# Phase integers summed in PSUM, transforms in 64x64 blocks, finer transposes and a new order, in a gated mix of S4D convolution and GLU

## The chip, the cores and the metric

One core of a Trainium2 chip runs the kernel. The metric is device time in microseconds (us). Before the change three runs took 764.48, 769.40 and 765.78 us; the median is 765.78.

## The reference

The input u is 2048 positions x 448 channels. Two branches read it, and a gate per position mixes them.

```python
# branch A: a state space model as a long convolution
dt = jnp.exp(log_dt)
A = -jnp.exp(log_A_real) + 1j * A_imag          # [448, 256]
C = (C_real + 1j * C_imag) * dt[:, None]
P = jnp.exp((A * dt[:, None])[:, :, None] * pos[None, None, :])
K = 2.0 * jnp.einsum("dn,dnl->dl", C, P).real   # [448, 2048]
Kf = jnp.fft.rfft(K, L2); Uf = jnp.fft.rfft(u_t, L2)
y = jnp.fft.irfft(Uf * Kf[None, :, :], L2)[:, :, :L]
a = y.transpose(0, 2, 1) + u * D_skip
# branch B: a gated linear unit, F = 1792
b = (sigmoid(x @ w_gate) * (x @ w_up)) @ w_down
g = sigmoid((u * gate_w).sum(-1, keepdims=True))
out = g * a + (1 - g) * b
```

In the kernel x of branch B is the same u.

## The kernel before

Everything is written as a list of operations, each with its engine, an estimated cost, the tiles that it reads and writes, and a priority. A planner (`Plan.order`) then simulates the five queues with these costs and hands out, at each moment, the ready operation of lowest rank; the table `RANK` overrides the priority for an engine, a tile name and a stage, and a tuple spreads several values over the operations of one kind. The result is a fixed program for each queue: TensorE (PE), VectorE (DVE), ScalarE (ACT), GpSimd (POOL) and SyncE (SP), which issues nearly all transfers in that order.

**GLU.** Weights and inputs are split into a rounded part (fp32r) and a remainder, and each product is three matmuls (L1180 to L1185 up, L1197 to L1199 down). ACT makes the rounded parts (L1154) and the tanh (L1168), DVE the remainders (L1156, L1172), the gating (L1169) and the running sum (L1213). This work depends on little else, so the planner uses it to fill PE during all stages.

**K.** For 28 chunks of 16 channels (`kgen`), `half_chunk` makes phases, cosines, sines and powers, and contracts them over the 256 states on PE in four column strips (L1075). In `turns` (L1002) PE turns six rows of phase digits into turns with a 96x128 by 512 matmul (L1010), ACT rounds them by adding and subtracting a large number (L1020, L1021, tile nn), and the integers are taken off. In this kernel PE does the first matmul a second time as the start of a new sum in the same PSUM bank, and adds nn through an identity matrix (L1025). ACT then takes the absolute value and the sine from the bank.

**Convolution.** A `Chain` (L551) holds one half of the channels (224) as x, 128 partitions x 32 x 224. Four of them run: two for u, whose spectra `us` go to DRAM, and two for K. Each has a first stage with twiddles (`stage1`, L599), a transposition of 32x32 blocks (by DRAM for three chains, by DVE for the last, L613), and a second stage. The second stage goes pair by pair (`spectrum_pair`, L624): four matmuls of 128 rows to 64 columns and 224 moving columns (L631), with a matrix that holds two 64x64 blocks and zeros. For u, ACT copies the result to x. For K, `product_pair` (L657) multiplies it with u's spectrum, loaded pair by pair into `ua`, on DVE into `ub` (L660), subtracts and adds the complex parts (L665, L666), and makes the inverse of the second stage with 64 rows to 128 columns (L674); ACT copies that to x. After another transposition, `back` (L680) makes the last matmuls (L711) and adds the result, times the gate, to the GLU's (L715). The tile pool of the products, `fk`, opens only when K's pool is done, so both chains of K have their products after the last chunk of K, in the last 200 us.

The matrices of the second stage, with a line each for the old forward and inverse blocks:

```python
m = np.zeros((128, 384), np.float32)
m[re, kr], m[im, kr] = cw, sw
m[kr, ir], m[ki, ir] = cw, -sw
```

Of the kernel before, what the change touches and what calls it, by code (L numbers as in the profile page):

```python
# [29 lines left out]
    ('Act', 'aci', 10): 301.5,  # L30
    ('Act', 'acr', 10): 451.5,
    ('Act', 'acr', 19): 236.5,
    ('Act', 'ci', 10): -166,
    ('Act', 'ci', 19): -194,
    ('Act', 'dots', 2): 332,
    ('Act', 'ec', 20): (66, -97, 126.5, 20, 20, 122.5, 20, 49.5),
    ('Act', 'ex1', 10): 1,
    ('Act', 'ex1', 19): 79,
    ('Act', 'fr', 20): (83.5, 83.5, -162, 49, 105, 90, 90, 20),
    ('Act', 'fx', 30): 244,  # L40
    ('Act', 'fx', 40): 275,
    ('Act', 'hh', 5): (5, -38.5, -38.5, 233, 233),
    ('Act', 'hh', 21): (108.5, 21, 21, -12, -12, -12),
    ('Act', 'hh', 45): 250,
    ('Act', 'hi', 10): -56.5,
    ('Act', 'nn', 20): (20, -251, -142.5, -142.5, -19, -247.5, 66, -161.5),
    ('Act', 'sg', 5): (5, 5, 310.5, 310.5, 5),
    ('Act', 'sg', 21): 99,
    ('Act', 'sg', 45): -123.5,
    ('Act', 'th0', 10): 264.5,  # L50
    ('Act', 'th0', 19): 194,
    ('Act', 'vh', 5): -355,
    ('Act', 'wh', 21): 139,
    ('Act', 'wh', 45): 123.5,
    ('Act', 'xs', 5): -263,
    ('DVE', 'aci', 19): -179.5,
    ('DVE', 'acr', 19): 545,
# [27 lines left out]
    ('DVE', 'uax', 40): (40, -67),  # L85
    ('DVE', 'ubx', 40): 250,
# [1240 lines left out]
```

## Time and profile before

| | us, or share |
|---|---|
| median of three runs | 765.78 |
| lowest, highest run | 764.48, 769.40 |
| span of the profiled execution, first to last instruction | 763.4 |
| VectorE idle in the span | 106.2 |
| ScalarE idle in the span | 234.1 |
| share of 16 DMA engines' span that queue q1's packets took | 54.9% |

The profile gives the span of its execution and no other time of it; the runs' times hold what lies before the first and after the last instruction as well. Busy times add up an engine's instructions where they do not overlap. On TensorE instructions overlap in its pipeline, so a mean duration there is longer than what one instruction takes from the engine. A row of the page's groups names line, engine, operation, written tile <- read tiles, shape and count, then busy us and mean ns of one, then the idle time ahead of them and who ended it.

### The profile page before, as it was taken

What the parts mean: (1) busy time and instruction counts of PE and PEld (TensorE: products, weight loads), DVE (VectorE), ACT (ScalarE), POOL (GpSimd) and SP (SyncE); (2) the same over time, 40 slices, a digit from 0 to 9 for tenths busy, and PEclk for the clock granted to TensorE, in tenths of its full rate; (3) what the DMA queues carried; (4) which work ended last, traced back from release to release, by engine and by line L of the source; (5) the groups of instructions that cost most, each with busy time, mean ns of one, the idle gap of its engine ahead of it and who ended that gap; (6) DMA issues with size and microseconds to landing.
All of it is one profiled execution on the core that took longest, in us unless ns stands there. A gap on an engine that the chain in (4) does not pass through costs nothing.

```text
span 763.4 us, 17397 instructions
## 1 busy us (share of the span) xinstructions
PE 728.4 (95%) x6996; PEld 552.5 (72%) x6996; DVE 657.2 (86%) x903; ACT 529.3 (69%) x994; POOL 231.4 (30%) x282
## 2 busy tenths in 40 slices
PE   4999999999999999999999999999998979999976
PEld 3878887777876877786677777778786757776743
DVE  5999898999999999999798989999964487677795
ACT  5579466899899899999899998898932513322100
POOL 0033225545554443435447535564000000000000
PEclk9999999999999999999999999999999999999998
DMA  8848417634882645596871359020149612335946
GB/s 274 207 114 221 126 50 208 156 116 142 191 160 107 197 127 179 199 195 183 281 190 62 123 165 183 20 77 14 39 94 235 206 43 73 122 121 152 196 133 168
DMA packets 97960, 111.59 MB, mean 146 GB/s; under 512 B 31032, under 2 KB 84984, under 8 KB 97368
## 3 DMA queue, kind: packets, MB, share of 16 engines
q1 hardware_dynamic: 97624, 110.03, 54.9%
q8 instruction: 55, 0.90, 0.5%
q0 software_dynamic: 256, 0.46, 0.2%
q14 instruction: 25, 0.20, 0.1%
HBM read 74.22 MB, written 36.24 MB: 145 GB/s over the span
## 4 chain that ended last, share of the span: by engine, by line
PE 63%; DMA 14%; DVE 8%; ACT 8%; POOL 2%; SPq 2%; issue 2%; DVEq 0%; ACTq 0%; POOLq 0%
PE gu_gps L1180 7%; PE gu_gps L1181 6%; PE gu_gps L1182 6%; PE dn_gps L1197 5%; DMA fx_fu<-shf 5%; PE tp_egp L1010 5%; PE kp_egp L1075 5%; PE dn_gps L1198 4%; PE dn_gps L1199 4%; PE fps_fups L631 4%; DVE fx_fk L613 2%; SPq L498 2%; PE gu_gps L1184 2%; PE gu_gps L1185 2%; PE tp_egp L1025 2%; PE fps_fups L599 2%
## 5 line engine op out<-in xcount | busy, mean ns | idle before, releaser
L1180 PE MATMUL gu_gps<-xs_glu,wh_glu 128*128 128x512 f32 x336 | 136.4, 406 | 15.3 <-ACT wh_glu L1154 10.5
L1181 PE MATMUL gu_gps<-xs_glu,wh_glu 128*128 128x512 f32 x336 | 133.1, 396 | 0.0
L1182 PE MATMUL gu_gps<-xs_glu,wl_glu 128*128 128x512 f32 x336 | 132.8, 395 | 0.0
L1049 DVE TENSOR_TENSOR es_eg<-tb_eg 128x1024 f32<-128x1024 f32 x112 | 110.1, 1001 | 10.8 <-PE kp_egp L1075 7.0
L1010 PE MATMUL tp_egp<-pos_sb,ph_eg 96*128 96x512 f32 x224 | 93.7, 429 | 1.1 <-ACT fr_eg L1028 0.6
L1197 PE MATMUL dn_gps<-vh_glu,hh_glu 128*128 128x448 f32 x224 | 88.0, 393 | 2.0 <-DVE ob_glu L1213 1.8
L1180 PEld LDWEIGHTS gu_gps<-xs_glu,wh_glu 128*128 128x128 f32 x336 | 64.0, 191 | 33.7 <-ACT wh_glu L1154 10.5
L996 POOL TENSOR_TENSOR tb_eg<-tb_eg 128x96 f32<-128x96 f32 (+2 forms) x84 | 83.9, 1003 | 6.2
L1198 PE MATMUL dn_gps<-vh_glu,hl_glu 128*128 128x448 f32 x224 | 82.4, 368 | 0.9 <-DVE hl_glu L1172 0.8
L1199 PE MATMUL dn_gps<-vl_glu,hh_glu 128*128 128x448 f32 x224 | 82.0, 366 | 0.0
L1021 ACT ACTIVATE nn_eg<-fr_eg 128x512 fp32r<-128x512 f32 x112 | 74.6, 666 | 5.8 <-PE tp_egp L1025 5.4
L1027 ACT ACTIVATE ec_eg<-tp_egp 128x512 f32<-128x512 f32 x112 | 70.3, 630 | 8.0 <-PE tp_egp L1025 7.5
L1182 PEld LDWEIGHTS gu_gps<-xs_glu,wl_glu 128*128 128x128 f32 x336 | 63.9, 190 | 14.9 <-DVE wl_glu L1156 0.5
L1181 PEld LDWEIGHTS gu_gps<-xs_glu,wh_glu 128*128 128x128 f32 x336 | 64.0, 191 | 11.9
L1028 ACT ACTIVATE fr_eg<-tp_egp 128x512 f32<-128x512 f32 x112 | 70.5, 630 | 2.0 <-PE tp_egp L1025 1.9
L1069 DVE TENSOR_TENSOR es_eg<-fr_eg,es_eg 128x1024 f32<-128x1024 f32 x56 | 71.3, 1274 | 0.1
L1067 DVE TENSOR_TENSOR ec_eg<-ec_eg,es_eg 128x1024 f32<-128x1024 f32 x56 | 70.8, 1264 | 0.2
L1168 ACT ACTIVATE sg_glu<-gu_gps 128x512 f32<-128x512 f32 x56 | 34.3, 613 | 50.0 <-PE gu_gps L1185 49.8
L1020 ACT ACTIVATE fr_eg<-tp_egp 128x512 f32<-128x512 f32 x112 | 65.3, 631 | 2.9 <-DVE es_eg L1069 2.0
L986 POOL MEMSET tb_eg<- 128x96 f32 x28 | 7.8, 286 | 193.9 <-DVE es_eg L1049 190.3
L1042 ACT ACTIVATE ec_eg<-ec_eg,half_pi 128x1024 f32<-128x1024 f32 x56 | 66.1, 1180 | 0.2
L1213 DVE SCALAR_TENSOR_TENSOR ob_glu<-dn_gps,og,ob_glu 128x448 f32<-128x448 f32 x72 | 48.8, 678 | 12.0 <-PE dn_gps L1199 11.9
(158 smaller groups left out, 1528.7 us busy)
## 6 DMA issues: line engine op xcount, KB each, us to landing
shf<-fx_fu SPq DMA_DIRECT2D x16, 896.0 KB
fx_fu<-shf SPq DMA_DIRECT2D x16, 896.0 KB
xr_glu<-in_w_dram SPq DMA_DIRECT2D x52, 256.0 KB
us<-fx_fu SPq DMA_DIRECT2D x4, 1792.0 KB
vr_glu<-in_w_dram SPq DMA_DIRECT2D x28, 224.0 KB
gt_pre<-in_u_dram SPq DMA_DIRECT2D x8, 448.0 KB
fx_fu<-in_u_dram SPq DMA_DIRECT2D x16, 224.0 KB
kd<-ke_eg SPq DMA_DIRECT2D x8, 448.0 KB
```

The costliest lines, as they stand in the source:

```text
L996: pool(96 * m, lambda n=n, m=m: G.tensor_mul(g3(n + 1, m), g3(1, m), g3(n, 1).to_broadcast([128, 32, 3, m])))
L1010: T.matmul(tp.real, ph[:, c % 2, 128 * nh:128 * nh + 128].bitcast(F32R), pos[:, 512 * i:512 * i + 512], start=True, stop=last)
L1021: op("Act", c_act(512), lambda: S.activation(nn.real, fi(), AF.Copy, scale=-1.0, bias=MAGIC), [(fr, i)], [nn], prio)
L1049: V.tensor_mul(o.rearrange("p d (i k) -> p d i k", k=ny), x.unsqueeze(3).to_broadcast([128, 16, nx, ny]), y.unsqueeze(2).to_broadcast([128 ...
L1067: op("DVE", c_dve(1024), lambda: V.tensor_mul(ec[:, :, 32:96], ec[:, :, 32:96], es[:, :, 32:96]), [(es, 1), (es, 2)], [(ec, "p")], prio)
L1069: op("DVE", c_dve(1024), lambda: V.tensor_mul(es[:, :, 32:96], fr.real, es[:, :, 32:96]), [fr], [(es, 1), (es, 2)], prio)
L1180: T.matmul(p.real, wh[:, k, cs], x[:, k], start=(k == 0), stop=False)
L1181: T.matmul(p.real, wh[:, k, cs], x[:, 4 + k], start=False, stop=False)
L1182: T.matmul(p.real, wl[:, k, cs], x[:, k], start=False, stop=False)
L1197: T.matmul(p[:, :D], hh[:, ts], vh.real, start=(i == 0), stop=False)
L1198: T.matmul(p[:, :D], hl[:, ts], vh.real, start=False, stop=False)
L1199: T.matmul(p[:, :D], hh[:, ts], vl.real, start=False, stop=(i == len(fs) - 1))
```

## The change

Five things change.

- `turns`: the second run of L1010 is gone. The first matmul's bank is kept, and the identity matmul adds nn onto it.
- The second stage takes two pairs at a time: four matmuls of 64 rows to 64 columns with 448 moving columns, each in its own quarter of the array, into two banks. The matrix shrinks from 128x384 to 128x192.
- The product loads u's spectrum with the real parts on both halves of the rows (c = 0) and the imaginary parts likewise (c = 1), multiplies in place, and lets the inverse matmuls add the two with a turned matrix. `ub`, the subtraction and the addition are gone. Four transfers of 224 KB load a group of two pairs, where two loaded it before. `ua` has 2 buffers instead of 3.
- The transposition on VectorE runs in 8 pieces of 28 channels instead of 4 of 56.
- The planner's costs change (64x64 blocks, column operands, POOL, some matmuls), and `RANK` grows from 84 entries to one for nearly each kind of operation.

```diff
-SU = dict(ft=1, ua=1, ub=1)
-SX = {'ft': 1, 'ua': 3, 'ub': 1, 'fps': 2}
-SK = {'ft': 2, 'ua': 3, 'ub': 1, 'fps': 3}
+SU = dict(ft=1)
+SX = {'ft': 1, 'ua': 2, 'fps': 2}
+SK = {'ft': 2, 'ua': 2, 'fps': 3}
...
+    re, im = slice(0, 32), slice(32, 64)
+    m = np.zeros((2, 64, 3, 64), np.float32)
+    fwd, inv, turned = m[0, :, 0], m[0, :, 1], m[0, :, 2]
+    fwd[re, re], fwd[im, re], fwd[re, im], fwd[im, im] = cw, sw, -sw, cw
+    inv[re, re], inv[im, re], inv[re, im], inv[im, im] = cw, -sw, sw, cw
+    turned[re], turned[im] = inv[im], -inv[re]
+    m[1] = m[0]
+    m = m.reshape(128, 192)
...
+def c_mm64(n, count=1):
+    return [(FOURTHS, 1.6667 * n + 30.0)] * count
...
-                for b in range(4):
+                for b in range(8):
                     def f(b=b):
-                        v = x[:, :, 56 * b:56 * b + 56].rearrange("p l d -> p d l")
+                        v = x[:, :, 28 * b:28 * b + 28].rearrange("p l d -> p d l")
                         V.transpose(v, v)
...
-        def spectrum_pair(self, r):
-            p = self.psum()
+        def spectrum_four(self, b):
+            p = [self.psum(), self.psum()]
             def f():
-                for c in range(2):
+                for z in range(2):
                     for i in range(2):
-                        T.matmul(p[64 * i:64 * i + 64, c * HD:c * HD + HD], m_sb[:, 64 * c:64 * c + 64],
-                                 self.x[:, 2 * r + i], start=True, stop=True)
+                        rows, to = slice(64 * i, 64 * i + 64), slice(64 * (i ^ z), 64 * (i ^ z) + 64)
+                        T.matmul(p[z][to, :D], m_sb[rows, 0:64], self.pair(2 * b + z, rows), start=True, stop=True)
...
-            for r in range(16):
-                ua = self.tile("ua", (128, 2, HD))
-                dma(lambda ua=ua, r=r: ua.real, lambda r=r: us[:, 2 * r:2 * r + 2], 128 * 2 * HD * 4,
-                    [(us, r // 8)], [ua], self.prio)
+            for b in range(8):
+                ua = self.tile("ua", (128, 2, 2, D))
+                for c in range(2):
+                    for g in range(2):
+                        dma(lambda ua=ua, c=c, g=g: ua[64 * g:64 * g + 64, c].rearrange("p z f -> p (z f)"),
+                            lambda b=b, c=c, g=g: us[64 * g + 32 * c:64 * g + 32 * c + 32, 4 * b:4 * b + 4].rearrange(
+                                "k l d -> k (l d)").unsqueeze(0).to_broadcast([2, 32, 2 * D]),
+                            64 * 2 * D * 4, [(us, b // 4)], [(ua, (c, g, 0)), (ua, (c, g, 1))], self.prio, HALF)
...
-            op("DVE", c_dve(2 * D, False), lambda: V.tensor_mul(
-                ub.real, ua.real.unsqueeze(2).to_broadcast([128, 2, 2, HD]),
-                p[:, :D].rearrange("p (c d) -> p c d", c=2).unsqueeze(1).to_broadcast([128, 2, 2, HD])), [ua, p], [ub], prio)
-            def add():
-                V.tensor_sub(x[:, 2 * r], ub[:, 0, 0], ub[:, 1, 1])
-                V.tensor_add(x[:, 2 * r + 1], ub[:, 0, 1], ub[:, 1, 0])
+            for z in range(2):
+                op("DVE", c_dve(2 * D, False), lambda z=z: V.tensor_mul(
+                    ua[:, :, z], ua[:, :, z], p[z][:, :D].unsqueeze(1).to_broadcast([128, 2, D])),
+                   [p[z]], [(ua, (c, g, z)) for c in range(2) for g in range(2)], prio)
...
-                        T.matmul(z[i][:, :HD], m_sb[rows, 128 + 128 * c:256 + 128 * c], x[rows, 2 * r + c],
-                                 start=c == 0, stop=c == 1)
+                    for z in range(2):
+                        for i in range(2):
+                            rows, to = slice(64 * i, 64 * i + 64), slice(64 * (i ^ z), 64 * (i ^ z) + 64)
+                            T.matmul(y[z][to, :D], m_sb[rows, 64 + 64 * c:128 + 64 * c], ua[rows, c, z],
+                                     start=c == 0, stop=c == 1)
-            for i in range(2):
-                evac(lambda i=i: x[:, 2 * r + i], z[i], [(x, r)], prio, HD)
+            for z in range(2):
+                evac(lambda r=2 * b + z: self.pair(r), y[z], [(x, 2 * b + z)], prio)
...
-        def x(last):
-            T.matmul(tp.real, ph[:, c % 2, 128 * nh:128 * nh + 128].bitcast(F32R),
-                     pos[:, 512 * i:512 * i + 512], start=True, stop=last)
-        op("PE", c_mm(512), lambda: x(True), [ph, pos], [tp], prio)
+        op("PE", c_mm(532), lambda: T.matmul(
+            tp.real, ph[:, c % 2, 128 * nh:128 * nh + 128].bitcast(F32R), pos[:, 512 * i:512 * i + 512], start=True, stop=True),
+           [ph, pos], [tp], prio)
...
-        def g():
-            x(False)
-            T.matmul(tp.real, idn.real, nn.real, start=False, stop=True)
-        op("PE", c_mm(512, 2), g, [nn, idn, ph, pos], [tp], prio)
+        op("PE", c_mm(532), lambda: T.matmul(tp.real, idn.real, nn.real, start=False, stop=True, skip_group_check=True),
+           [nn, idn], [tp], prio)
```

More of the change, by code (lines that the diff above doesn't have):

```diff
@@ L86 @@
-    ('DVE', 'ubx', 40): 250,
[27 rows of a table removed]
+    ('Act', 'aci', 10): (-502.5, -363.5),
+    ('Act', 'aci', 19): (-352, 754.5),
+    ('Act', 'acr', 10): (264.5, -368.5, 327),
+    ('Act', 'acr', 19): (729, -700, 800),
+    ('Act', 'ai', 10): -534,
+    ('Act', 'ai', 19): 764,
+    ('Act', 'bsx0', 10): (666, 876),
+    ('Act', 'bsx0', 19): (782, 900),
+    ('Act', 'ci', 10): (689, 173.5, 70),
+    ('Act', 'ci', 19): (25, -391.5, -252.5),
+    ('Act', 'cr', 10): -40,
+    ('Act', 'cr', 19): 549.5,
+    ('Act', 'dots', 1): -419,
@@ new lines @@
+    ('Act', 'dots', 2): -700,
+    ('Act', 'dots', 16): (-78.5, 29),
[14 rows of a table added]
+    ('Act', 'junk', 10): (-404, 388.5),
+    ('Act', 'junk', 19): (-233, -242, -215),
[28 rows of a table added]
+    ('DVE', 'aci', 10): -159.5,
+    ('DVE', 'aci', 19): 19.5,
+    ('DVE', 'acr', 10): -438,
+    ('DVE', 'acr', 19): 655.5,
+    ('DVE', 'ai', 10): -223,
+    ('DVE', 'ai', 19): -40.5,
+    ('DVE', 'bsx0', 10): (-179.5, -174.5),
+    ('DVE', 'bsx0', 19): (-613, 104.5),
+    ('DVE', 'ci', 10): -339,
+    ('DVE', 'ci', 19): -673.5,
+    ('DVE', 'cr', 10): (-561, -429),
@@ L114 @@
+    ('DVE', 'gt', 2): (-301, -580, -690, -614),
+    ('DVE', 'gt', 16): (-169, 813.5, 353, 163.5, -700, -492, 381, 232.5),
+    ('DVE', 'half_pi', 0): 300,
[20 rows of a table added]
+    ('DVE', 'ones', 10): -119.5,
[6 rows of a table added]
+    ('DVE', 'skip', 20): 888,
[5 rows of a table added]
+    ('DVE', 'uax', 40): (840.5, 515, -52, 130.5, -446, -688, 378.5, 896.5),
[26 rows of a table added]
+    ('Pool', 'idn', 1): -436.5,
+    ('Pool', 'pos_sb', 10): 465,
[57 rows of a table added]
 }
 WB, ECB, FRB, TPB, KPB, GUB, FPS, SGB, XRB = 3, 2, 2, 2, 1, 2, 2, 3, 5
-SU = dict(ft=1, ua=1, ub=1)
+SU = dict(ft=1)
 XR0 = 7
 MOVE = True
-SX = {'ft': 1, 'ua': 3, 'ub': 1, 'fps': 2}
@@ L520, in gated_mix @@
     skip = const([128, 2, 56], "skip")
-    m_sb = const([128, 384], "m_sb")
+    m_sb = const([128, 192], "m_sb")
     half_pi = const([128, 1], "half_pi")
@@ L676, in product_pair @@
-            op("PE", c_mm4(HD, 2, ROWS), f, [(x, r), m_sb], z, prio)
-            for i in range(2):
-                evac(lambda i=i: x[:, 2 * r + i], z[i], [(x, r)], prio, HD)
+                    for z in range(2):
[3 more added lines that the diff above has]
+                                     start=c == 0, stop=c == 1)
@@ L1212, in glu_down @@
         o = ob[H, j]
-        op("DVE", c_dve(D, False), lambda: V.scalar_tensor_tensor(
+        op("DVE", c_dve(D, False, column=True), lambda: V.scalar_tensor_tensor(
             o.real, p[:, :D], og[:, c:c + 1], o.real, op0=ALU.mult, op1=ALU.add), [p, (og, c)], [o], prio)
```

97 lines of the change are left out of this document (33 added, 64 removed), and 210 rows, old and new, of the table RANK.

## The prediction

> **What bounds the kernel now.** I read the page first, then the busy time of each engine by stage, then the chain of waits and the order of time on TensorE. The page:
>
> ```profile
> span 763.4 us, 17397 instructions
> ## 1 busy us (share of the span) xinstructions
> PE 728.4 (95%) x6996; PEld 552.5 (72%) x6996; DVE 657.2 (86%) x903; ACT 529.3 (69%) x994; POOL 231.4 (30%) x282
> ```
>
> TensorE leaves 35 us of 763.4 idle, so an instruction taken from it is worth about its pace there, as long as other work can move up. Whether it can is told by the stages: start, parameters, generation of K (140 to 564 us), and the tail with the two inverse transforms. Columns: stretch, its length, then busy us (and count) of PE, PE weight loads, DVE, ACT, POOL, then granted clock, DMA share, GB/s.
>
> ```profile
> 0.00:20.00 20.00, 9.52 (x32) 7.40 (x33) 11.52 (x31) 11.70 (x19) 1.46 (x6) 1.00 0.89 275
> 20.00:140.00 120.00, 118.89 (x541) 99.17 (x540) 110.13 (x197) 80.70 (x146) 39.10 (x42) 1.00 0.59 152
> 140.00:564.00 424.00, 419.39 (x5317) 317.82 (x5316) 399.62 (x473) 388.42 (x714) 190.84 (x234) 1.00 0.53 139
> 564.00:764.00 200.00, 180.62 (x1112) 128.08 (x1110) 135.91 (x204) 48.46 (x117) 0.00 (x0) 0.97 0.57 145
> ```
>
> In the K stage PE is full (419.4 of 424), but VectorE is close behind: 399.6, only 24.4 us of room. In the tail PE has 19.4 us of holes and DVE 64 us of room. The pace of a matmul is not its duration (they overlap); it is the distance of starts, read from the order of time on PE (start, us, instruction):
>
> ```profile
> 157.79 0.40 PE L1010 MATMUL tp_egp<-pos_sb,ph_eg 96*128 96x512 f32 x1
> 158.03 0.40 PE L1025 MATMUL tp_egp<-nn_eg,idn 128*128 128x512 f32 x1
> 158.27 0.40 PE L1184 MATMUL gu_gps<-xs_glu,wh_glu 128*128 128x512 f32 x1
> ```
>
> Each 512-column matmul takes PE 0.24 us. For the small f32 matmuls the chain of waits gives whole groups (start, time that the group holds PE):
>
> ```profile
> 224.58 1.66 PE fps_fups L631 x16
> 227.37 1.03 PE kp_egp L1075 x64
> 228.40 0.91 PE fps_fups L631 x8
> ...
> 580.68 5.21 DMA uax_fk<-us
> ...
> 634.79 0.96 PE fps_fups L674 x8
> ```
>
> Eight records of L631 are one pair of the second transform stage: four matmuls of 224 columns, two records each. One pair alone holds PE 0.91 us; the second of two adds 1.66 - 0.91 = 0.75. So 0.16 goes into entering and leaving the tiling, and 0.75 us is two rounds of 224 columns with two column halves at work.
>
> **The change part by part.** Counts first (busy us, mean ns):
>
> ```profile
> L1010 PE MATMUL tp_egp<-pos_sb,ph_eg 96*128 96x512 f32 x224 | 93.7, 429 | 1.1 <-ACT fr_eg L1028 0.6 <-ACT ec_eg L1027 0.3 <-ACT fr_eg L1020 0.2
> ...
> L631 PE MATMUL fps_fups<-fx_fu,m_sb 128*64 128x224 f32 x384 | 44.3, 363 | 2.0 <-DMA ph_eg<-phd 0.7 <-DMA fx_fu<-shf 0.7 <-ACT fx_fu L549 0.5
> ...
> L674 PE MATMUL fps_fups<-fx_fu,m_sb 64*128 64x224 f32 x128 | 16.2, 372 | 3.7 <-DVE fx_fu L665 3.7
> L674 PE MATMUL fps_fkps<-fx_fk,m_sb 64*128 64x224 f32 x128 | 15.6, 362 | 0.0
> L631 PE MATMUL fps_fkps<-fx_fk,m_sb 128*64 128x224 f32 x128 | 15.3, 360 | 0.0
> ```
>
> 1. *Phase integers.* 112 tiles of turns run L1010 twice, once to round and once more, to be added to L1025. The second goes: 112 x 0.24 = 26.9 us of PE, all in the K stage. No wait is added: L1025 waited for ScalarE's nn before, and the bank was held from the first matmul to the sine before too.
>
> 2. *Second stage in 64x64 blocks.* (384 + 128) / 8 = 64 pairs cost between 64 x 0.83 (two together) = 53.1 and 64 x 0.91 = 58.2; I take 55. Now two pairs are one group of four matmuls of 448 columns, each on its own quarter of the array. If the four run at once, a group is one round of 448 columns, 0.75 + 0.16 = 0.91: 32 x 0.91 = 29 us, a gain of 26. If only two run at once: 1.66 each, 53.1, a gain of 0 to 5, say 2. If none overlap, 3.16 each, 101, a loss of 46. No row shows the quarters. The nearest for the good end is L1075: 32 matmuls of 64 columns in 1.03 us; at 0.75/448 us a column they would take 3.4 us one by one and 0.86 four at a time, so four column strips do run at once. L674 shows two row halves at once (its four matmuls of 224 columns in 0.96). As both axes overlap alone, I take four at once.
>
> A rule of the Trainium skill speaks against it: "TensorEngine Tiling (Array Packing)", Restrictions and Gotchas, says that different row tiles cannot access the same PSUM bank simultaneously, and here the upper and lower rows of one group write halves of one bank. No run here shows what the chip does then; by this rule the second price above would hold, and the sum would be that of rival B.
>
> 3. *Inverse.* 64 x 128 blocks become 64 x 64. 32 pairs x 0.96 = 30.7 us before; 16 groups of two rounds, 1.50 + 0.21 = 1.71, are 27.4 after: a gain of 3.3; two at a time 3.21, 51.4, a loss of 20.7.
>
> So PE loses 26.9 + 26 + 3.3 = 56 us. Half the pairs (the transforms of u) lie in the K stage: 26.9 + 13 = 40 there, 16 in the tail.
>
> 4. *The product on VectorE.* The complex add and subtract go into the inverse matmul's accumulation. Four groups of 16 like these leave:
>
> ```profile
> L666 DVE TENSOR_TENSOR fx_fu<-ubx_fk 128x224 f32<-128x224 f32 x16 | 6.2, 387 | 0.0
> L665 DVE TENSOR_TENSOR fx_fk<-ub_fk 128x224 f32<-128x224 f32 x16 | 6.2, 386 | 0.1
> ```
>
> 64 x 0.386 = 24.7 us, all in the tail. The multiplications stay 32 of 896 elements; their rows (median ns, then first and last start):
>
> ```profile
> L660 DVE TENSOR_TENSOR ubx_fk<-uax_fk,fps_fups x16: 1080/1087/1090, 586.0 to 693.4; 128x896 f32<-128x896 f32 x16
> L660 DVE TENSOR_TENSOR ub_fk<-ua_fk,fps_fkps x16: 1080/1086/1090, 632.2 to 714.1; 128x896 f32<-128x896 f32 x16
> ```
>
> The last product starts 714.1 - 632.2 = 82 us after its chain's first. A group of the new kind is serially 0.91 + 2 x 1.09 + 1.71 = 4.8 us, so eight are 38; with the last group's run I say 41. From 564 to 632 (K to DRAM, first stage, transposes) and from 714 to the end (transposes, back, stores) little changes: 68 + 41 + 49 = 158 us is the floor of the tail by its chain.
>
> 5. *Loads.* The 32 loads of u's spectrum, 224 KB each, become 64, in four parts a group, and now wait for the group before last to leave its inverse matmuls (2 buffers for 3). Behind a waiting load on SP stand the weight loads of the GLU, and behind those PE. One such load took 5.2 us in the chain above at 580, when K came back from DRAM. I count nothing, hidden by the other chain's group and by GLU matmuls; without that cover see rival C.
>
> 6. *Transposes.* Eight pieces in place of four:
>
> ```profile
> L613 DVE STREAM_TRANSPOSE fx_fk<-fx_fk 128x1792 f32<-128x1792 f32 x8 | 29.0, 3621 | 0.0
> ```
>
> Eight more instructions cost from below zero (a short GLU step may slip between pieces and feed PE) up to one fixed cost each. That is 0.15 us by the rows of point 4: (1.086 - 0.386) / (896 - 224) is 1.04 ns an element, and 0.386 - 224 x 1.04 ns leaves 0.15. 8 x 0.15 = 1.2 us; I take 1, in the slack of the rounding. ScalarE's evacuations of the inverse halve in number; it has 151 us of room in the tail.
>
> 7. *Order.* Ranks and durations decide which ready instruction goes first, on every queue. I price it by the room: at best it recovers part of the 35 us that PE idles, at worst it fails to use what is freed.
>
> **The sum.** In the K stage PE's 40 us are worth something only if GLU work moves up. The GLU's cost on DVE:
>
> ```profile
> L1213 DVE SCALAR_TENSOR_TENSOR ob_glu<-dn_gps,og,ob_glu 128x448 f32<-128x448 f32 x72 | 48.8, 678 | 12.0 <-PE dn_gps L1199 11.9
> ...
> L1172 DVE TENSOR_TENSOR hl_glu<-sg_glu,hh_glu 128x512 fp32r<-128x512 f32 x56 | 40.0, 726 | 2.6 <-ACT hh_glu L1171 2.6
> L1169 DVE SCALAR_TENSOR_TENSOR sg_glu<-sg_glu,gu_gps 128x512 f32<-128x512 f32 x56 | 38.4, 686 | 14.3 <-PE gu_gps L1185 14.1
> L1156 DVE TENSOR_TENSOR wl_glu<-xr_glu,wh_glu 128x512 fp32r<-128x512 f32 x52 | 37.3, 746 | 1.1 <-ACT wh_glu L1154 1.0
> ...
> L1156 DVE TENSOR_TENSOR vl_glu<-vr_glu,vh_glu 128x448 fp32r<-128x448 f32 x28 | 19.9, 712 | 3.6 <-ACT vh_glu L1154 3.4
> ```
>
> Together 184.4 us, against PE's sums for the same tiles (gu, then dn):
>
> ```profile
> sum 764.00, PE 322.63 PEld 231.53 DVE 38.41 ACT 34.34; mean PE 80.66 PEld 57.88 DVE 9.60 ACT 8.58
> sum 764.00, PE 168.18 PEld 121.70 DVE 48.85 ACT 10.69; mean PE 42.05 PEld 30.43 DVE 12.21 ACT 2.67
> ```
>
> That is 184.4 / 490.8 = 0.38 us of DVE for each us of PE. The tail can give away only so much: 180.6 - 16 = 164.6 of PE work plus today's 19.4 of holes is 184, and its floor is 158, so 26 us move up. They cost DVE 9.9, which stands then at 409.5 of 424. The other 14 us of PE room could shorten the K stage, if DVE can be packed closer. It can at times:
>
> ```profile
> 520.00:540.00 20.00, 20.00 (x269) 16.29 (x266) 19.90 (x25) 17.32 (x33) 7.68 (x9) 1.00 0.05 14
> ```
>
> At 98% the 409.5 need 418 us, 6 less. So the span falls to 564 + 158 = 722 without that and 716 with it; I take 717. The median of the runs, 765.8, stands 2.4 above the profiled span, so 717 + 2.4 is **719 us**.
>
> **The rivals.** *A, VectorE takes over.* The K stage stays 424 long and nothing moves up, as DVE's 24 us of room is scattered in waits that PE's release does not fill. Only the tail gains, 16 us: 763.4 - 16 + 2.4 = 750. For: DVE at 94% over the stage. Against: the 20 us above at 99.5%, and PE full now, so GLU work stands ready.
>
> *B, the quarters run two at a time.* Gain 26.9 + 2, loss 20.7, net 8: 758. For: both row halves of a group write one bank, and no row has both axes. Against: strips and halves that overlap now.
>
> *C, slower: the loads bound the product.* Sixteen groups' loads, from 586 on. A load as at 580.68, 5.2 us, and three more behind it at the tail's 145 GB/s, 1.6 each, is 10.0. If two buffers hide none of it, 16 x 10 = 160, the product ends at 746, and 49 us follow: 795 + 2.4 = 797. It gets slower than now from (714 - 586) / 16 = 8 us a group. Against: two chains alternate, and the DMA share of the tail is 0.57.
>
> *D, the order wins more:* half of the 35 idle us come back on top, 717 - 17 = 700 of span, 702 with the 2.4. For: the tail's holes of 19.4 us and the 10.5 of the start are order and latency. Against: DVE, which has less and less room.
>
> **How the numbers follow.** Forecast 0.65, A 0.13, B 0.06, C 0.06, D 0.10. The forecast's own range is 707 (all 56 us, 763.4 - 56) to 735 (half of the moved work fails); D reaches down to 697 and A up to 750, so 697 to 750 holds the forecast, most of D and half of A, about 0.8. One per cent (7.7 us) is about what a measurement tells from no change. Faster: forecast, A, D, a little of B: 0.88. Same: most of B, 0.06. Slower: C, 0.06.
>
> **What would show it.** L1010 x112. L631's successor in 32 groups of about 0.9 us, and records of four blocks that start within some ns; starts 0.7 us apart would show B. No add or subtract on DVE. The K stage at DVE 97% with PE below 97%: the forecast; DVE at 94% with PE at 90%: A. Products that wait for the DMA of ua: C. Wrong altogether if the first 140 us move by more than 5, since only the order touches them.

## The result and the profile after

The changed kernel takes 933.98 us (median of four runs, 931.37 to 935.85), the kernel before 765.13 (762.56 to 769.40). The ratio is 1.2217, with a 95% interval of 1.2164 to 1.2269: slower by 22%, where 719 us were forecast. The page after begins so:

```profile
span 933.3 us, 16571 instructions
...
PE 725.2 (78%) x6628; PEld 511.4 (55%) x6628; DVE 639.6 (69%) x847; ACT 525.2 (56%) x962; POOL 232.5 (25%) x282
...
PE   4999988999999998899998996774233442553797
```

Each digit of the last line is a fortieth of the span, 23.3 us. TensorE is nearly full for 24 slices, some 560 us, as it was before, and from the 28th to the 37th it is busy for a fifth to a half of the time. The stages, with the columns of the table in the prediction:

```profile
140.00:564.00 424.00, 406.29 (x5055) 296.61 (x5055) 397.87 (x474) 383.13 (x707) 188.06 (x233) 0.97 0.54 142
564.00:934.00 370.00, 198.60 (x996) 117.54 (x994) 118.33 (x151) 45.85 (x86) 0.00 (x0) 0.76 0.31 94
```

All the loss is in the tail, which grew from 199 to 370 us with PE busy for little more than half of it. A stretch in the middle of the tail shows what was moving:

```profile
740.00:760.00 20.00, 5.46 (x27) 1.97 (x27) 2.68 (x3) 1.02 (x2) 0.00 (x0) 0.66 0.13 53
```

All compute engines are nearly still, and the DMA share, the mean over 16 engines, is 0.13: 0.13 x 16 = 2.1, the work of two engines out of sixteen. The chain of waits names who moves (start, us, step; SPq is SyncE's queue):

```profile
697.02 4.19 SPq L614
701.25 4.20 SPq L614
705.49 4.19 SPq L614
...
729.52 21.88 DMA ua_fk<-us
751.52 1.10 DVE ua_fk L781
752.67 3.77 PE fps_fkps L791 x16
```

L614 is the helper that issues every transfer from SP. The loads of u's spectrum leave it one every 4.2 us. VectorE and TensorE wait for the buffer, work for 5 us, and wait again. The issues by destination, after (count: min, median, max ns, first and last start):

```profile
L614 SPq DMA_DIRECT2D uax_fk<-us x32: 482/2637/8859, 562.6 to 822.6; - x32
L614 SPq DMA_DIRECT2D ua_fk<-us x32: 483/4193/8859, 601.0 to 852.4; - x32
```

And before, where one load brought the 224 KB of one pair over all 128 rows (the changed kernel fetches every row twice, so with the number of these loads their bytes doubled too):

```profile
L498 SPq DMA_DIRECT2D uax_fk<-us x16: 319/322/432, 580.7 to 676.1; - x16
L498 SPq DMA_DIRECT2D ua_fk<-us x16: 319/320/430, 582.1 to 700.8; - x16
```

An issue that took 0.32 us now holds the queue for up to 8.9, and 64 loads last from 562.6 to 852.4, 4.5 us each. The view of waits gives who stood still for it, in us, times, and the longest:

```profile
DVE ua_fk L781 <- DMA ua_fk<-us: 82.3, 6, 21.0
DVE uax_fk L781 <- DMA uax_fk<-us: 78.5, 6, 23.6
...
ACT vh_glu L1268 <- DMA vr_glu<-in_w_dram: 71.7, 8, 52.2
```

The last row is the GLU: its weights stand behind the loads on SP's queue, so even the work that could have filled PE was locked out.

### The profile page after: what moved, and what is told of

It reads as the page before. It is cut to its first block, busy times and chain, and to the rows that moved or that the text cites. A ratio compares the mean times of both kernels' runs of the same rounds, so it can differ in the third digit from the quotient of the medians.

```text
span 933.3 us, 16571 instructions
## 1 busy us (share of the span) xinstructions
PE 725.2 (78%) x6628; PEld 511.4 (55%) x6628; DVE 639.6 (69%) x847; ACT 525.2 (56%) x962; POOL 232.5 (25%) x282
## 4 chain that ended last, share of the span: by engine, by line
PE 39%; DMA 21%; SPq 18%; ACT 11%; DVE 6%; issue 3%; POOL 1%; DVEq 0%; ACTq 0%
SPq L614 18%; PE gu_gps L1294 5%; PE kp_egp L1189 4%; DMA uax_fk<-us 4%; PE gu_gps L1295 4%; PE gu_gps L1296 4%; DMA vr_glu<-in_w_dram 4%; PE dn_gps L1311 4%; DMA xr_glu<-in_w_dram 3%; PE dn_gps L1312 3%; PE dn_gps L1313 3%; DMA ua_fk<-us 2%; PE tp_egp L1126 2%; PE tp_egp L1139 2%; DMA fx_fu<-shf 2%
## 5 line engine op out<-in xcount | busy, mean ns | idle before, releaser
L1163 DVE TENSOR_TENSOR es_eg<-tb_eg 128x1024 f32<-128x1024 f32 (+1 forms) x112 | 107.2, 982 | 8.3 <-PE kp_egp L1189 5.0
L1294 PEld LDWEIGHTS gu_gps<-xs_glu,wh_glu 128*128 128x128 f32 x336 | 64.2, 191 | 42.2 <-ACT sg_glu L1282 11.5
L791 PE MATMUL fps_fkps<-ua_fk,m_sb 64*64 64x448 f32 x128 | 28.4, 854 | 71.6 <-DVE ua_fk L781 66.7
L781 DVE TENSOR_TENSOR uax_fk<-uax_fk,fps_fups 128x896 f32<-128x896 f32 x16 | 17.0, 1083 | 86.2 <-DMA uax_fk<-us 78.5
L781 DVE TENSOR_TENSOR ua_fk<-ua_fk,fps_fkps 128x896 f32<-128x896 f32 x16 | 16.7, 1083 | 82.6 <-DMA ua_fk<-us 82.3
L1142 ACT ACTIVATE fr_eg<-tp_egp 128x512 f32<-128x512 f32 x112 | 70.0, 628 | 1.8 <-PE tp_egp L1139 1.8
```

The lines of the kernel that those rows point to most:

```text
L1163: V.tensor_mul(o.rearrange("p d (i k) -> p d i k", k=ny), x.unsqueeze(3).to_broadcast([128, 16, nx, ny]), y.unsqueeze(2).to_broadcast([128 ...
L1294: T.matmul(p.real, wh[:, k, cs], x[:, k], start=(k == 0), stop=False)
```

## The experiments

### The loads

**Both halves as plain transfers.** In the changed kernel each load of 64 rows is made by two transfers of 32 rows, in the same place of the queue. The bytes, the buffers and the order stay.

```diff
-  us[64 * g + 32 * c:64 * g + 32 * c + 32, ...].rearrange("k l d -> k (l d)").unsqueeze(0).to_broadcast([2, 32, 2 * D])
+  for r in range(2):
+      nc.sync.dma_start(
+          ua[64 * g + 32 * r:64 * g + 32 * r + 32, c].rearrange("p z f -> p (z f)"),
+          us[64 * g + 32 * c:64 * g + 32 * c + 32, 4 * b:4 * b + 4].rearrange("k l d -> k (l d)"))
```

> The changed kernel with each load of u's spectrum issued as two plain transfers of 32 rows, one for each copy, in place of one transfer whose source has a leading dimension of 2 with step 0; plan, order, buffers and bytes stay. Theory 1 (the leading dimension of 2 puts a transfer on 2 of the 16 DMA engines: in the changed kernel's profile the DMA share stays at 0.13, that is 2.1 of 16, and a load of 224 KB takes 4.2 us): the loads take about 1 us each, the SP queue stops being the chain, the stretch from 640 to 880 us shrinks by some 64 x 3.2 = 205 us, and the time falls to 700 to 735. Theory 2 (two buffers in place of three, and the order on SP, hold the products up): the products still wait, and the time stays over 880. Theory 3 (a transfer into fewer partitions is slow): the halves get slower still, over 930.

Measured: 738.38 us, a ratio to the kernel before of 0.9651 (0.9624 to 0.9679). One line of access pattern was worth 934 - 738 = 196 us and turned the sign of the whole change. The issues of the loads in this kernel (a count twice as high, of half the size):

```profile
L774 SPq DMA_DIRECT2D uax_fk<-us x64: 302/419/940, 562.8 to 662.0; - x64
L774 SPq DMA_DIRECT2D ua_fk<-us x64: 302/419/1541, 586.9 to 670.1; - x64
```

All 128 are out by 670 instead of 852. So neither the number of loads, nor their bytes, nor the two buffers, nor the new order made the stall. The time is 3 us above the range of theory 1; what is missing is taken up below.

**Leading dimension of four.** One load brings all 128 rows of a half as four copies of 32 rows.

```diff
-  for g in range(2):
-      ... .unsqueeze(0).to_broadcast([2, 32, 2 * D])
+  ... .unsqueeze(0).to_broadcast([4, 32, 2 * D])
```

> Two transfers a group in place of four: the source has a leading dimension of 4 with step 0 and 32 rows behind it, and fills all 128 rows (the upper half gets the lower half's spectrum, which leaves that half of the channels' data wrong in the product; bytes stay the same). Theory 1: 4 of 16 engines work, so a load of 448 KB takes about 4.2 us again, the DMA share in the products is about 0.25, and the 134 us that are saved bring the time to about 800 (780 to 820). If reading the same rows again is what is slow, four reads of a row are no faster than two: 930 or more.

Measured: 820.67 us (one run), at the upper end of theory 1's range and less than 1 us above it. A load of 448 KB that stands right behind another holds the queue for some 4 to 5 us (4.42 at 676.9 us, 5.16 at 671.7), about what 224 KB took with a leading dimension of two. So the same bytes move faster with four than with two, and far slower than with the plain loads.

**Leading dimension of two without repetition.** The load keeps its shape, 2 x 32 rows, but the two parts come from different rows instead of from the same ones.

```diff
-  us[64 * g + 32 * c:64 * g + 32 * c + 32, ...].unsqueeze(0).to_broadcast([2, 32, 2 * D])
+  us.v("(e k) l d -> e k (l d)", e=2)[:, 32 * c:32 * c + 32, ...]
```

> The changed kernel with the same four transfers a group, the same 64 rows of destination and a leading dimension of 2, but with two different sets of 32 source rows, 64 rows apart, instead of the same set twice (the product then takes u's spectrum of both halves where it should take one half twice). Theory 1: nothing changes, 4.2 us a load, 930 +- 10. If the step of 0, the repeated reading of one row, is what is slow: the loads take about 1 us and the time is near 720.

Measured: 933.66 us (one run), the time of the changed kernel to 0.4 us. Reading a row twice costs nothing here; it is the size of the outermost dimension that counts.

**The same load in the kernel before.** To see whether the changed kernel's surroundings matter, the kernel before got its loads in this form; nothing else in it changed.

```diff
-  dma(lambda ua=ua, r=r: ua.real, lambda r=r: us[:, 2 * r:2 * r + 2], ...)
+  for g in range(2):
+      nc.sync.dma_start(
+          ua[64 * g:64 * g + 64].rearrange("p a d -> p (a d)"),
+          us[64 * g:64 * g + 32, 2 * r:2 * r + 2].rearrange("k l d -> k (l d)").unsqueeze(0).to_broadcast([2, 32, D]))
```

> The kernel before with each load of u's spectrum for the product made as two transfers of 64 rows whose source has a leading dimension of 2 with step 0; the imaginary rows are replaced by a copy of the real ones, so this part of the computation is changed. Theory 1 (such a transfer is spread over 2 of the 16 engines): each of the 64 transfers takes 2.4 to 4.2 us instead of half of 0.3 us, the queue of the loads paces the product, and the time lies at 789 to 900 us. The rival (the loads cost what they did only because of the changed kernel's buffers and order): within 10 us of 765.

Measured: 835.48 us (one run), 70 us slower than before. Its issues (L655):

```profile
L655 SPq DMA_DIRECT2D uax_fk<-us x32: 482/638/3555, 581.5 to 733.9; - x32
L655 SPq DMA_DIRECT2D ua_fk<-us x32: 482/2138/5030, 589.8 to 760.6; - x32
```

The median of the second group, 2.14 us for 112 KB, is half of 4.19 for 224 KB: 52 and 53 KB a microsecond. That is somewhat less than the 2.4 us that were expected at least; the time lies in the expected range. The last load starts at 760.6 instead of 700.8, and the end moves by 70. That settles the cause: the shape of the access pattern, in either kernel.

The Trainium skill states this, in "DMA: Bandwidth & Descriptors", Rules for kernel authors: how many of the 16 engines a transfer uses is set by the outermost dimension of its access patterns that is not 1, so a leading broadcast of c copies holds it to at most c engines. The trace agrees (a DMA share of 0.13, the work of 2.1 engines, for c = 2), and the run without repetition shows the same for a leading dimension that is no broadcast.

### Why the kernel with plain loads takes 738 us and not 719

With the loads mended, 19 us are still missing. The page and the stages of that kernel:

```profile
span 736.1 us, 16688 instructions
...
PE 691.5 (94%) x6628; PEld 497.8 (68%) x6628; DVE 639.8 (87%) x847; ACT 525.0 (71%) x962; POOL 233.3 (32%) x282
```

```profile
140.00:564.00 424.00, 406.31 (x5050) 296.49 (x5049) 398.04 (x472) 382.95 (x706) 188.21 (x233) 0.96 0.53 141
564.00:764.00 200.00, 164.82 (x997) 104.10 (x995) 117.77 (x151) 45.16 (x86) 0.00 (x0) 0.98 0.69 174
```

Idle time of PE is 736.1 - 691.5 = 44.6 us, and the forecast had 717 - (728.4 - 56) = 44.6 as well (in other stages, as the end of "Why the prediction was wrong" shows; that the sums agree is chance). What differs is PE's busy time: it fell by 36.9 instead of 56. And the K stage has a granted clock of 0.96 where it had 1.00. To see which lines are short, the time that each line's matmuls hold PE (from a start to the next one, or to the matmul's own end) was summed from the trace, with the part of it that starts where the record of the granted clock says 0.5:

| us on PE (of it at half clock) | before | plain loads | fell by | forecast |
|---|---|---|---|---|
| phases and integers | 91.9 (0) | 72.0 (6.8) | 19.9 | 26.9 |
| second stage | 55.3 (0.7) | 31.7 (5.7) | 23.6 | 26 |
| inverse | 28.5 (0) | 25.7 (0) | 2.8 | 3.3 |
| everything else | 552.7 (5.9) | 562.1 (18.7) | -9.4 | 0 |
| sum | 728.4 (6.6) | 691.5 (31.2) | 36.9 | 56 |

Work at half clock takes twice its time, so (31.2 - 6.6) / 2 = 12.3 us of the 19.1 are the clock. Theory G: gaps in PE's work, too short to matter by themselves, halve the clock. PE in order of time shows where they come from (start, us, instruction, in brackets the idle time ahead of it and who ended it):

```profile
352.31 0.49 PE L1142 MATMUL tp_egp<-nn_eg,idn 128*128 128x512 f32 x1 [0.42 <-ACT nn_eg L1140]
353.75 0.49 PE L1142 MATMUL tp_egp<-nn_eg,idn 128*128 128x512 f32 x1 [0.94 <-ACT nn_eg L1140]
354.72 0.50 PE L1129 MATMUL tp_egp<-pos_sb,ph_eg 96*128 96x512 f32 x1 [0.48 <-ACT fr_eg L1145]
355.69 0.50 PE L1129 MATMUL tp_egp<-pos_sb,ph_eg 96*128 96x512 f32 x1 [0.47 <-ACT fr_eg L1145]
...
358.95 1.77 PE L748 MATMUL fps_fups<-fx_fu,m_sb 64*64 64x448 f32 x8
```

Four holes of 0.4 to 0.9 us, each a wait for ScalarE; from 356.7 to 363.5 the clock is 0.5, and the group of the second stage takes 1.77 us instead of 0.98. The identity matmul L1142 must wait for ScalarE's nn. In the kernel before the repeated first matmul stood in just that place, with its operands long ready.

**Filling the holes.** Repeated phase matmuls, which write the same result once more, stand ahead of L1142 in the eight tiles whose holes came before a halving. The queues' order is that of the kernel with plain loads on every engine.

```diff
+        fill = {8: 4, 58: 2, 59: 3, 60: 2, 67: 3, 100: 2, 103: 2, 104: 3}.get(4 * c + 2 * nh + i, 0)
+        def g():
+            for _ in range(fill):
+                T.matmul(tp.real, ph[...], pos[...], start=True, stop=True)
+            T.matmul(tp.real, idn.real, nn.real, start=False, stop=True, skip_group_check=True)
```

> The kernel with plain loads, with 23 repeated phase matmuls (each 512 columns, overwriting the same result) placed ahead of the identity matmul of eight tiles, where TensorE was idle in front of the places at which the granted clock halved; the order of the queues is kept. Theory G (the short idle gaps halve the clock, some 34 us of the span run cold, and that costs up to 17 us): the cold windows behind these tiles vanish, the clock goes from 0.976 to about 1.0, 726 to 735 us although there is 23 x 0.24 = 5.5 us more TensorE work. Theory P (the clock is a side matter, TensorE's work sets the time): 738 plus 0 to 5, so 738 to 743 us.

Measured: 733.24 us, a ratio to the kernel before of 0.9572 (0.9535 to 0.9610); without the filler it was 0.9651 (0.9624 to 0.9679). The matmuls are 21, not the 23 of the expectation: 5.0 us more work, and 5 us less time. The same place on PE:

```profile
352.31 0.50 PE L1148 MATMUL tp_egp<-nn_eg,idn 128*128 128x512 f32 x1 [0.19 <-ACT nn_eg L1140]
352.64 0.86 PE L1146 MATMUL tp_egp<-pos_sb,ph_eg 96*128 96x512 f32 x3
353.75 0.50 PE L1148 MATMUL tp_egp<-nn_eg,idn 128*128 128x512 f32 x1 [0.24 <-ACT nn_eg L1140]
354.71 0.50 PE L1129 MATMUL tp_egp<-pos_sb,ph_eg 96*128 96x512 f32 x1 [0.47 <-ACT fr_eg L1151]
355.68 0.50 PE L1129 MATMUL tp_egp<-pos_sb,ph_eg 96*128 96x512 f32 x1 [0.47 <-ACT fr_eg L1151]
...
358.64 0.98 PE L748 MATMUL fps_fups<-fx_fu,m_sb 64*64 64x448 f32 x8
```

The starts up to 354.7 are the same to 0.01 us, so nothing was sped up directly; but the clock holds, and the second stage's group takes 0.98. The clock of the K stage is 0.99:

```profile
140.00:564.00 424.00, 407.41 (x5085) 297.19 (x5086) 400.89 (x477) 383.20 (x708) 185.77 (x230) 0.99 0.55 144
```

PE time at half clock fell from 31.2 to 12.4 us, a gain of 9.4, against 5.0 of added work: 4.4, and the span fell by 5.0. PE's waits for nn in the K stage fell from 7.6 to 3.0 us. The time lies in theory G's range, so the short gaps and the clock that falls by them are shown as a cause. Not all of it went: at the filled tiles two halvings of 3.41 us are left, at 385.0 and 511.3 us, and there is one of 6.83 at 118.8, where the kernel with plain loads has none.

**All the work put back.** In the kernel with plain loads the phase matmul of the 112 tiles is issued twice in its own place, the order of the queues kept, so the 26.9 us that step 1 took out are back.

```diff
-  op("PE", c_mm(532), lambda: T.matmul(tp.real, ph[...], pos[...], start=True, stop=True), ...)
+  def g():
+      for _ in range(2 if on_pe else 1):
+          T.matmul(tp.real, ph[...], pos[...], start=True, stop=True)
+  op("PE", c_mm(532), g, ...)
```

> The kernel with plain loads, with the phase matmul of the 112 tiles issued twice in its place, so that the 112 x 0.24 = 26.9 us of TensorE work that the change took out are back, with the order of the queues kept. Theory P (in the new order TensorE's work is on the path, so the work taken out was worth its price): 738 + 27 = 765 us, 758 to 768. Theory G (the work taken out left gaps that halve the clock, which gave most of it back): the clock rises above 0.976, and the time stays between 738 and 755 us.

Measured: 745.91 us, a ratio to the kernel before of 0.9732 (0.9693 to 0.9772). In this order 26.9 us of TensorE work are worth 745.9 - 738.4 = 7.5 us (6.2 by the two ratios): theory G's range holds, and theory P's does not. Its page, against that of the plain loads above:

```profile
span 745.3 us, 16912 instructions
...
PE 706.9 (95%) x6740; PEld 516.0 (69%) x6740; DVE 641.8 (86%) x847; ACT 528.1 (71%) x962; POOL 219.9 (30%) x282
```

PE's busy time rose by 15.4 us only, 11.5 less than the work put back. The clock is 0.986 instead of 0.976: PE time at half clock fell from 31.2 to 16.5 us, which is 7.3 of the 11.5. Its idle time fell from 44.6 to 38.4: 15.4 - 6.2 = 9.2, the rise of the span. An earlier form of this run put the repeated matmul ahead of L1142 and declared its operands to the planner:

> The changed kernel with plain loads (738.4 us), order kept, but with L1010's second run put back in each of the 112 tiles of turns: 26.9 us more of TensorE work in the K stage, which that kernel's plan does not know of. Theory P: the K stage of TensorE is nearly full there (406 of 424 us busy), so the time rises by 10 to 27, to 748 to 765. Theory G: the holes are filled, the granted clock in the K stage rises from 0.96 to 1.00, and the time stays within 5 us of 738.

It took 782.64 us, a ratio of 1.0211 (1.0163 to 1.0259). But with other operands the planner had made another order on PE, SP, DVE and ACT, so that run does not price the matmuls: the 37 us between the two runs lie in the order and the place, since both have the same matmuls.

### The phase integers and the order

**Phase integers alone, order kept.** In the kernel before the repeated matmul goes and nothing else; all queues keep their order.

```diff
         def g():
-            x(False)
-            T.matmul(tp.real, idn.real, nn.real, start=False, stop=True)
+            T.matmul(tp.real, idn.real, nn.real, start=False, stop=True, skip_group_check=True)
```

> The kernel before, planned with its old costs so that every queue keeps its order, but without the second run of L1010 (the integers are added onto the first run's bank). It removes 112 x 0.24 = 26.9 us of TensorE work and nothing else. Theory P (the work is what counts, and the 813.75 us of the run with the phase integers alone came from the new order that the planner made): 740 to 766, never slower than before. Theory G (taking work from TensorE in the K stage opens holes, in which the granted clock falls: 0.91 over that stage in the run with the phase integers alone, 1.00 before): the clock of the K stage falls below 0.97 here too, and the time stays at 765 or goes above.

Measured: 764.42 us over ten runs, a ratio of 0.9974 (0.9945 to 1.0003): no change that this measurement shows. The clock of the K stage stays at 1.00, so theory G falls here. The K stage, and from the waits of the weight loads the row that took up the gain, before and now:

```profile
140.00:564.00 424.00, 408.13 (x5223) 298.98 (x5222) 400.99 (x476) 388.93 (x719) 193.65 (x234) 1.00 0.54 140
```

```profile
PEld tp_egp L1025 <- ACT nn_eg L1021: 4.3, 12, 0.8
```

```profile
PEld tp_egp L1024 <- ACT nn_eg L1021: 19.9, 39, 2.7
```

PE is busy 11 us less there (419.4 before), but in a kept order no matmul can pass another. It now waits 19.9 us for nn, at full clock, and K's last contraction starts only 2.9 us earlier (559.5 instead of 562.4).

**Phase integers alone, planned again.** The same edit with the operands and the cost told to the planner.

```diff
-        op("PE", c_mm(512, 2), g, [nn, idn, ph, pos], [tp], prio)
+        op("PE", c_mm(512), lambda: T.matmul(tp.real, idn.real, nn.real, start=False, stop=True, skip_group_check=True),
+           [nn, idn], [tp], prio)
```

> The kernel before with the phase integers alone: L1010 once per tile of turns and the integers added onto its bank; all ranks, costs of the other operations and the second stage stay as before. The prediction priced this at 112 x 0.24 = 26.9 us of TensorE in the generation of K. If TensorE bounds that stage and GLU work moves up, 740 to 752; if VectorE or ScalarE bounds it, 758 to 768; the ranks were not made for it, so an order that fits worse could give 765 to 780.

Measured: 813.75 us, a ratio of 1.0639 (1.0603 to 1.0674), with a clock of 0.91 in the K stage. Less work and 49 us more, outside all three of the ranges.

**Its order with the work put back.** The repeated matmul stands in that kernel again, the planner told nothing: the instructions of the kernel before in the other order.

```diff
-        op("PE", c_mm(512), lambda: T.matmul(tp.real, idn.real, nn.real, ...), [nn, idn], [tp], prio)
+        def g():
+            T.matmul(tp.real, ph[...], pos[...], start=True, stop=False)
+            T.matmul(tp.real, idn.real, nn.real, start=False, stop=True)
+        op("PE", c_mm(512), g, [nn, idn], [tp], prio)
```

> The kernel before in the order that the planner makes for it with the phase integers added in their bank (813.75 us with that change), but with the repeated phase matmul put back: the instructions of the kernel before, in another order of the queues. If the order itself costs those 49 us: 805 to 840 us, with the clock still near 0.91 in the transform's stage. If the work taken out left gaps that halve the clock: the repeated matmul fills them, the clock rises to 0.97 or more in that stage, and the time lies at 765 to 795 us.

Measured: 840.57 us, a ratio of 1.0958 (1.0905 to 1.1010). That is at the upper end of the first reading, by which the order itself costs the time; filling the gaps brought the clock of the K stage to 0.92 only. The same instructions cost 75 us more in another order, and there the 26.9 us of TensorE work are worth nearly all of their price: 840.6 - 813.8 = 26.8, or 24.4 by the two ratios. Where the 75 come from is read from the GLU's first matmuls (tile gu) by stage, before:

```profile
140.00:564.00 424.00, 165.68 (x618) 114.53 (x616) 19.04 (x28) 17.73 (x28) 1.00 0.53 139
564.00:840.00 276.00, 64.85 (x247) 46.50 (x247) 8.46 (x12) 6.57 (x11) 0.98 0.41 105
```

and in the other order:

```profile
140.00:564.00 424.00, 114.60 (x407) 77.53 (x405) 12.90 (x19) 11.06 (x18) 0.92 0.50 130
564.00:840.00 276.00, 118.95 (x459) 84.35 (x459) 14.51 (x21) 12.56 (x21) 0.96 0.46 120
```

Of the 618 gu matmuls that ran beside K a third (618 - 407 = 211) no longer does and is done afterwards, while K's contractions take as long as before (147.0 to 563.2 us). Which of the planner's choices makes K's holes there was not taken apart.

**Plain loads with the old ranks.** The kernel with plain loads, its `RANK` and costs set back to those of the kernel before.

```diff
-    return 0.833 * n + (50.0 if psum else 93.0) + (94.0 if column else 0.0)
+    return 0.833 * n + (50.0 if psum else 93.0) + (45.0 if column else 0.0)
...
-        op("PE", c_mm(532), lambda: T.matmul(tp.real, idn.real, nn.real, start=False, stop=True, skip_group_check=True),
+        op("PE", c_mm(512), lambda: T.matmul(tp.real, idn.real, nn.real, start=False, stop=True, skip_group_check=True),
```

> The changed kernel with plain loads, but with the ranks and the planner's costs of before (the cost of the 64x64 blocks stays, since before had none). Instructions and bytes are those of the 738.4 us run; only the order differs. If the new ranks are worth something for these instructions, the time is above 738, between 750 and 800 (the run with the phase integers alone under old ranks lost 49 us against before); if the order doesn't matter, 738 +- 5; if the new ranks are what keeps the kernel from the 719 that was forecast, below 733.

Measured: 780.08 us, a ratio of 1.0180 (1.0130 to 1.0229), with a clock of 0.92 in the K stage. With the old ranks and costs the changed instructions are no faster than the kernel before, as the first reading has it; the new ones are worth 780.1 - 738.4 = 41.7 us to them (40.5 by the two ratios). Ranks and costs were set back together, so their shares stay open.

## Why the prediction was wrong

The step that failed is step 5, the loads: "I count nothing, hidden by the other chain's group and by GLU matmuls". Where the prediction did price a load, in rival C, it went by the bytes and by rows of loads of another shape, 5.2 us for a first and 1.6 for the next. The shape itself was in the diff, a leading dimension of 2, and no row that the prediction shows is of such a load. A load of 224 KB measured 4.2 us, the four of a group 16.8 where 10 were priced, and nothing hides them: the GLU's weights wait in the same queue. Rival C had the mechanism (the loads bound the product), the sign and the threshold (8 us a group), at a chance of 0.06 and 797 us, but not what makes such a load slow. Most of its error of 137 us is that price: the 64 loads were issued over 289.8 us, 18.1 a group, and 16 x (18.1 - 10) = 130. The range did not reach to either.

With the loads mended the other steps can be judged one by one.

- *Step 1, phase integers*: in part. 112 matmuls went, but "No wait is added" was wrong in effect. The wait for nn was there before, covered by the repeated matmul; what was removed was partly work that cost nothing. The row of PE's waits for nn in the K stage, before and with plain loads (us, times, longest):

```profile
PE tp_egp L1025 <- ACT nn_eg L1021: 0.7, 2, 0.5
```

```profile
PE tp_egp L1142 <- ACT nn_eg L1140: 7.6, 10, 1.4
```

  What the 26.9 us are worth depends on the order: nothing that shows in the order before, 7.5 us in the new order, 26.8 in a third (6.2 and 24.4 by the ratios).
- *Step 2, second stage*: right. The chain of the kernel with plain loads gives 0.91 us for a group of two pairs, and 0.75 for one that follows in the same tiling:

```profile
618.16 1.66 PE fps_fups L794 x16
619.83 1.50 PE fps_fkps L794 x16
621.33 0.75 PE fps_fups L748 x8
...
630.46 0.91 PE fps_fups L748 x8
```

  All four quarters run at once, though upper and lower rows write halves of one bank. The rule of the Trainium skill, "TensorEngine Tiling (Array Packing)", Restrictions and Gotchas, does not hold for this case; the measurement decides, and rival B falls. 26 were forecast and 23.6 came; the half clock makes up the difference (5.7 - 0.7, halved, is 2.5).
- *Step 3, inverse*: right, 1.66 us or 1.50 a group against 1.71, and 2.8 of 3.3 us.
- *Step 4, the adds on VectorE*: gone as forecast. VectorE's busy time fell by 657.2 - 639.8 = 17.4 us net, less than 24.7 - 1.
- *Step 6, transposes*: 31.3 us in sixteen pieces against 29.0 in eight, so 2.3 more instead of 1; too small to matter.
- *Step 7, order*: mis-sized. "I price it by the room" set 35 us as the bound of the gain. But an order also decides whether room is used at all: orders of one set of instructions differed by 75 us, and of the changed set by 42. Rival D asked for 17 more on top by using PE's holes. In the tail it did come (PE idle there from 18.8 to 7.5 us), but the stages before it lost more than that, 7.4 ahead of K and 13.5 beside it.

*The sum.* The forecast let 26 us of GLU work move up out of the tail into a K stage that ends at 564 us, and shortened that stage by 6. The rows of K's last contractions, before and with plain loads (first and last start):

```profile
L1075 PE MATMUL kp_egp<-es_eg x1792: 219/219/243, 146.6 to 562.4; 128*32 128x64 f32 x200
```

```profile
L1192 PE MATMUL kp_egp<-es_eg x1792: 219/219/314, 135.7 to 546.9; 128*32 128x64 f32 x200
```

K ends 15.5 us earlier, but 10.9 of that are there when it begins: the stage itself takes 411.2 us instead of 415.8. From K's end to the span's end it takes 189.2 us instead of 201.0, 11.8 less; together 27.3, by which the span fell. Where the GLU's matmuls (tiles gu and dn) ran, counted in the trace from the first to the last contraction of K:

| GLU matmuls | ahead of K | beside K | after K |
|---|---|---|---|
| before | 562 | 921 | 421 |
| plain loads | 478 | 925 | 501 |

So this step of the sum failed as well: no GLU work to speak of moved up beside K, and 80 matmuls, some 19 us at 0.24 each, moved from ahead of K to the tail. K's earlier start is that shift and no gain by itself. The prediction had named it as a sign against it ("Wrong altogether if the first 140 us move by more than 5"), and so it is: the order did it, and step 7 had no term for it. The stage from K's first to its last contraction, before and with plain loads:

```profile
146.10:562.60 416.50, 411.89 (x5285) 311.98 (x5284) 393.45 (x465) 382.89 (x705) 190.84 (x234) 1.00 0.52 138
```

```profile
135.30:547.10 411.80, 393.74 (x5054) 285.76 (x5053) 395.11 (x465) 381.19 (x702) 192.09 (x234) 0.96 0.53 141
```

Of PE's 40 us of relief there, 4.7 shortened the stage, 13.5 became idle time (4.6 before, 18.1 now), and 14 went to the half clock, at which 27.9 us of its work ran. The other 8 were not taken apart.

Short gaps that halve the clock were in no term and in no rival; over the whole span they took 12.3 us of PE's time. The other 7 us by which PE's busy time missed the forecast lie in the phases' matmuls (3.6) and in everything else (3.0). For the phases part of the reason shows: at full clock 29 of their matmuls (18 before) stand beside a gap and hold PE for 0.46 us on average, where one in a row holds it for 0.28. For the rest it was not found.

Rival A had the outcome for the K stage, "nothing moves up", but its reason, VectorE taking over, is not shown. VectorE is busy for 395.1 of 411.8 us there, yet of the 17.2 us of PE's waits that the view lists for the K stage 16.2 end with ScalarE, and the kernel with the filler did the same VectorE work, 394.9 us, in a stage of 406.7. What bounds that stage with the loads mended stays open.

The best version here is the plain loads with the filler: 733.24 us, 0.9572 (0.9535 to 0.9610) of the time before.

## What to carry to other kernels

Read the outermost dimension of every access pattern in a diff before pricing its bytes: with 2 there, a load moved at the rate of two of sixteen engines, held its queue for 4.2 us instead of 0.3, and 64 of them turned a gain of 3.5% into a loss of 22%. Work taken from the busiest engine is worth its time only if what follows is ready; ask what the removed instruction was standing in front of, and whether the gap that it leaves lets the clock fall. A planned order belongs to its set of instructions and costs: judge an edit in a kept order and in a new one, since here the second alone moved the time by up to 75 us.

## What the runs showed of the hardware that was not expected

The clock of TensorE can fall by gaps far shorter than expected. In the record of the granted clock of the kernel with plain loads it halves for multiples of 3.41 us (five times before the end, 34 us). In the 3.41 us ahead of these halvings PE was idle for 1.33 to 1.78 us: once, ahead of 356.7 us, in three pieces of 0.44 to 0.48 that add up to 1.39, once mostly in two (0.93 and 0.47), and three times almost all in one gap of 1.30 to 1.78. In the rows shown, the four holes from 352 to 356 us add up to 2.3 us without the filler and the clock fell; with it they are 1.4 and the clock held.

Idle time alone does not decide it, though. In the same trace this gap of 3.26 us left the clock at 1:

```profile
119.23 0.50 PE L1297 MATMUL gu_gps<-xs_glu,wh_glu 128*128 128x512 f32 x1 [3.26 <-ACT sg_glu L1285]
```

The Trainium skill, "TensorE: Matmul & The Clock Gate", Why this matters for your kernels, advises no idle gaps over some 3 us between bursts; here gaps of about half of that, or pieces that add up to it, were enough to lose the clock, and one of 3.26 us did not lose it. Where the limit lies, and what else goes into it, was not measured by a run of its own.
